# Attention scores from block 3 on as two 128-row products a head, with the key transposes moved to the first head's score bank

## Chip, core and metric

The program runs on one core of one Trainium2 chip. The metric is device time in microseconds (us), from three runs of the kernel before and one profiled execution of it. The inputs are fixed: 4 sequences of 768 tokens, 8 heads of 64 channels, two mixture layers behind the attention.

## What is computed

```python
scores = scale * np.matmul(q, k.transpose(0, 1, 3, 2))      # [4, 8, 768, 768], scale = 1/8
keep = is_sink | in_window                                  # first 4 keys, and the last 128 up to the query
scores = np.where(keep, scores, -1000000000.0)
a = np.exp(scores - np.max(scores, axis=-1, keepdims=True))
a = a / (np.sum(a, axis=-1, keepdims=True) + 1e-09)
x = np.matmul(a, v)                                         # heads side by side: [3072, 512]
...
h = np.maximum(x @ w_in, 0.0)                               # [3072, 2048]
x = h * h @ w_out                                           # [3072, 512]
...
out[mask] = gate_w[mask, None] * eom[mask, e, None] * (np.maximum(x[mask] @ w1[e], 0.0) @ w2[e])
```

The last line runs over 8 experts, each on the tokens whose largest gate logit is its own. The change touches the scores alone.

## The kernel before

**Stages.** The 3072 tokens are cut into 12 blocks of 256 (`t`), three to a sequence. While TensorE multiplies block t-1 by `w_in` (`l1`, L610) and `w_out` (`l2`, L635), sixteen pieces a block, the attention of block t runs in between (`attn_events`, L585). From about 730 us on the experts follow. Every product of the large matrices is made of three: each float32 operand is split into a high part and a rest, and high times high, high times rest and rest times high are added up in the accumulator.

**One attention step.** A block has 8 steps: four pairs of heads (`p`), two halves of 128 queries each (`n`). A step has four parts. `scores` (L446) multiplies the queries by 256 keys and 4 sink keys: 260 columns, or 128 in the first half of a sequence's first block. VectorE adds the mask and finds the maximum (L469), ScalarE exponentiates (L472) and scales (L484). `ptrans` (L492) transposes the probabilities on TensorE, ScalarE and VectorE split them (L512, L513), and GpSimd cuts them into the two key blocks (L517). `pv` (L523) multiplies them by the values. `prep_k` (L366) and `prep_q` (L395) bring the keys and queries of a pair into columns by transposes on TensorE, once for its two steps, and split them.

**The 64-row products.** A head has 64 channels, so a pair fills 128 rows, the first head on rows 0 to 63, the second on 64 to 127. From block 2 on (`T32`) a step's scores are three products for each head, in turns of first and second head, each over 64 rows:

```python
for m, (a_, b_) in enumerate(((0, 0), (0, 1), (1, 0)) if t >= T32 else ()):
    for e in range(2):
        r = slice(64 * e, 64 * e + 64)
        PE.matmul(ps[e][:, 0:W], lhsT=qt[r, a_, n, :], rhs=kt[r, b_, c0:c0 + W], start=(m == 0), stop=(m == 2))
```

**Accumulator banks.** `ps[0]` and `ps[1]` of a step lie in the banks `s0` and `s1`, one buffer each. The query transposes use `s0` too. The key transposes (`psk_`), the probabilities' (`pspt`), the sink sums' (`psst`, `fin_sink`, L557) and the gate's pieces (`psg`) share the one bank `T`. `pv` and the sink's correction (`add_sink`, L565) share the bank `O`.

**Order.** A sorted list of events sets where the attention's parts fall. A step's scores stand every fourth half-piece; `LEADS` (L36) says how far ahead of them the key and query transposes stand, and how far behind the probabilities' transposes and `pv`. `run_to` (L859) takes the due events once after each `l1` and once after each `l2`. A scheduler then sets the order on the other engines.

Of the kernel before, what the change touches and what calls it, by code (L numbers as in the profile page):

```python
# [8 lines left out]
F32 = mybir.dt.float32  # L9
F32R = mybir.dt.float32r  # L10
# [3 lines left out]
AF = mybir.ActivationFunctionType  # L14
ALU = mybir.AluOpType
# [31 lines left out]
def kern(ctx, tc, q, k, v, n_sink, window, w_in, w_out, w_gate, w_og, w1, w2, out):  # L47
    nc = tc.nc
    V, A, G, PE, SY = nc.vector, nc.scalar, nc.gpsimd, nc.tensor, nc.sync
# [16 lines left out]
    psS = ps1.enter_context(tc.tile_pool(name="psS", bufs=1, space=PSUM))  # L66
    psT = ps1.enter_context(tc.tile_pool(name="psT", bufs=1, space=PSUM))
# [7 lines left out]
    ident = const.tile([128, 128], F32, name="ident")  # L75
# [193 lines left out]
    att = attS.enter_context(tc.tile_pool(name="att", bufs=2, side="right"))  # L269
# [96 lines left out]
    def prep_k(t, p):  # L366
        o = 1 if t % 3 == 0 else 0
        x = nat.pop(("k", t, p))
        ps = psT.tile([128, 4, 128], F32, tag="T", name="psk_")
        if t == 0:  # L370
            fill(ps[:].rearrange("p n c -> p (n c)"), 1)
        for n in range(o, 3):
            PE.transpose(ps[:, n], x[:, n].rearrange("p h d -> p (h d)"), ident[:])
        kt = att.tile([128, 2, KS * 3], F32R, tag="kT", name="kT", bufs=2)
        kv = kt[:].rearrange("p a (n c) -> p a n c", c=KS)
        if t < T32:
            kf = kv[:, 0].bitcast(F32)
# [9 lines left out]
        A.activation(out=kv[:, 0, o:3, 0:128], in_=ps[:, o:3], func=AF.Copy)  # L387
        V.tensor_tensor(out=kv[:, 1, o:3, 0:128], in0=ps[:, o:3], in1=kv[:, 0, o:3, 0:128].bitcast(F32), op=ALU.subtract)
        if o:
            G.tensor_copy(out=sk[:, p], in_=kv[:, :, 1, 0:NS].bitcast(F32))  # L390
        for n in range(o, 2):
            G.tensor_copy(out=kv[:, :, n, 128:KS], in_=sk[:, p].bitcast(F32))
        kTt[t, p] = kt

    def prep_q(t, p):  # L395
        x = nat.pop(("q", t, p))
        if t < T32:
            ps = psO.tile([128, 4, 128], F32, tag="O", name="psq")
        else:
            ps = psS.tile([128, 260], F32, tag="s0", name="psq")[:, 0:256].rearrange("p (n c) -> p n c", n=2)  # L400
# [4 lines left out]
        o = att.tile([128, 2, 2, 128], F32R, tag="qT", name="qT", bufs=2)  # L405
        qTt[t, p] = o
        if t < T32:
            if p % 2:
                A.activation(out=o[:, 0].bitcast(F32), in_=ps[:, 0:2], func=AF.Copy)
            else:  # L410
                V.tensor_copy(out=o[:, 0].bitcast(F32), in_=ps[:, 0:2])
            Vt[t, p] = nat.pop(("v", t, p))
            more(t, p)
            return
        A.activation(out=o[:, 0], in_=ps[:, 0:2], func=AF.Copy)
        V.tensor_tensor(out=o[:, 1], in0=ps[:, 0:2], in1=o[:, 0].bitcast(F32), op=ALU.subtract)
# [29 lines left out]
    def scores(t, p, n):  # L446
        i = 2 * (t % 3) + n
        W = 128 if i == 0 else 260
        c0 = KS * n if i else KS
        mask = (M0, M1, M2)[min(i, 2)]  # L450
        qt = qTt[t, p]
        kt = kTt[t, p]
        if t == 0 and n % 2:
            ps = [psX.tile([128, 512], F32, tag=f"x{e}", name=f"psx{e}") for e in range(2)]
        else:
            ps = [psS.tile([128, 260], F32, tag=f"s{e}", name=f"pss{e}") for e in range(2)]
        if t == 0:
            fill(ps[0][:, 0:W], 2)
        for e in range(2 if t < T32 else 0):
            r = slice(64 * e, 64 * e + 64)  # L460
            PE.matmul(ps[e][:, 0:W], lhsT=qt[r, 0, n, :].bitcast(F32), rhs=kt[r, 0, c0:c0 + W].bitcast(F32), start=True, stop=True)
        for m, (a_, b_) in enumerate(((0, 0), (0, 1), (1, 0)) if t >= T32 else ()):
            for e in range(2):
                r = slice(64 * e, 64 * e + 64)
                PE.matmul(ps[e][:, 0:W], lhsT=qt[r, a_, n, :], rhs=kt[r, b_, c0:c0 + W], start=(m == 0), stop=(m == 2))  # L465
# [89 lines left out]
    skT = {}  # L555

    def fin_sink(t):  # L557
        ps = psT.tile([128, 4, 128], F32, tag="T", name="psst")
        for n in range(2):
            PE.transpose(ps[:, n], psk[n][:].rearrange("p h c -> p (h c)").bitcast(F32), ident[:])  # L560
        o = att.tile([128, 2, 128], F32R, tag="pskT", name="pskT", bufs=1)
        A.activation(out=o[:], in_=ps[:, 0:2], func=AF.Copy)
        skT[t] = o
# [21 lines left out]
    def attn_events(t):  # L585

        ev = []
        h0 = 32 * (t - 1) - 8
        a0, a1, a2, a3 = LEADS[min(t, 2)]
        for p in range(4):  # L590
            ev.append((h0 + 8 * p - a0, lambda p=p: prep_k(t, p)))
            ev.append((h0 + 8 * p - a1, lambda p=p: prep_q(t, p)))
        for n in range(8):
            ev.append((h0 + 4 * n, lambda n=n: scores(t, n // 2, n % 2)))
            ev.append((h0 + 4 * n + a2, lambda n=n: ptrans(t, n // 2, n % 2)))
            ev.append((h0 + 4 * n + a3, lambda n=n: pv(t, n // 2, n % 2)))
# [594 lines left out]
```

## Time and profile before

| | |
|---|---|
| median of 3 runs | 1150.73 us (1150.65 to 1150.94) |
| profiled execution, its own time | 1149.8 us |
| its span, first to last instruction | 1148.1 us |
| TensorE busy (matmuls) | 1120.3 us, 98% |
| VectorE, ScalarE, GpSimd busy | 727.9 us (63%), 637.6 us (56%), 417.0 us (36%) |
| granted TensorE clock, mean of the span | 0.995 |

PE stands for TensorE, PEld for its weight loads, DVE for VectorE, ACT for ScalarE, POOL for GpSimd. A matmul's busy time includes the way of its data through the array, so neighbouring matmuls overlap in the records: what one costs the next is read from start to start, not from its length. A share of the whole span mixes stages, so the stretch that the change touches has to be read for itself. L12 is line 12 of the kernel.

### The profile page before, as it was taken

To read this page: it belongs to the slowest core of one execution; us is meant where nothing else is said; L and a number is where in the kernel's file an instruction comes from. 1 tells how busy PE (TensorE), PEld (TensorE's weight loads), DVE (VectorE), ACT (ScalarE), POOL (GpSimd) and SP (SyncE) were. 2 spreads that over 40 slices of the span, in tenths; PEclk is the share of its full clock that TensorE was granted. 3 is DMA by queue.
4 is the path that set the end of the run, shared out by engine and by line. 5 is a ranking of instruction groups with operands and counts; after the bars stand their busy time and mean duration, and the time that the engine had idled before them with its cause. 6 is when DMAs were issued, how large, how long until landed. Compare 5 with 4: busy or idle time off the path is not lost. (4 is left out here: it accounts for less than half of the span.)

```text
span 1148.1 us, 23733 instructions
## 1 busy us (share of the span) xinstructions
PE 1120.3 (98%) x7002; PEld 941.3 (82%) x7002; DVE 727.9 (63%) x2027; ACT 637.6 (56%) x1749; POOL 417.0 (36%) x917
## 2 busy tenths in 40 slices
PE   7999999999999999999999999999999999999995
PEld 4556788888888888888888888997788888888884
DVE  4899877576766666676667676557412576764153
ACT  4898766777676767676767767454232232232200
POOL 3112563256564336565325655310211112221111
PEclk9999999999999999999999999999999999999998
DMA  6687111121211111211112110296411456653110
GB/s 154 179 234 211 39 24 46 39 54 34 54 29 50 38 45 38 56 28 44 36 38 56 38 31 1 28 253 162 129 39 47 155 185 218 220 206 134 48 45 24
DMA packets 139392, 100.08 MB, mean 87 GB/s; under 512 B 103908, under 2 KB 112228, under 8 KB 139239
## 3 DMA queue, kind: packets, MB, share of 16 engines
q1 hardware_dynamic: 131476, 82.28, 25.8%
q0 software_dynamic: 5472, 14.19, 3.7%
q10 hardware_dynamic: 2290, 1.84, 0.5%
q8 instruction: 64, 1.05, 0.4%
q14 instruction: 90, 0.73, 0.3%
HBM read 85.56 MB, written 13.76 MB: 87 GB/s over the span
## 5 line engine op out<-in xcount | busy, mean ns | idle before, releaser
L619 PE MATMUL psh<-xT,WI 128*128 128x256 f32 x2112 | 284.8, 285 | 0.0
L619 PEld LDWEIGHTS psh<-xT,WI 128*128 128x128 f32 x2112 | 270.6, 190 | 9.7 <-issue 0.4
L956 PE MATMUL psh<-WI,xt 128*128 (+1 forms) x672 | 162.1, 395 | 1.0 <-ACT xt L936 0.7
L629 DVE TENSOR_TENSOR r<-r 128x256 f32<-128x256 f32 x180 | 82.3, 458 | 116.8 <-ACT r L622 116.7
L644 PE MATMUL psx<-WOb,h 128*128 128x512 f32 x576 | 154.0, 404 | 0.8 <-ACT h L631 0.5
L956 PEld LDWEIGHTS psh<-WI,xt 128*128 128x128 f32 x672 | 123.8, 188 | 26.8 <-ACT xt L936 1.4
L644 PE MATMUL psx<-WOa,h 128*128 128x512 f32 x528 | 143.4, 406 | 0.0
L644 PEld LDWEIGHTS psx<-WOb,h 128*128 128x128 f32 x576 | 101.8, 188 | 19.9 <-ACT h L631 1.4
L472 ACT ACTIVATE P<-P,st 128x260 f32<-128x260 f32 (+1 forms) x192 | 93.8, 489 | 42.8 <-DVE st L469 42.7
L972 DVE TENSOR_TENSOR ht<-psht,ht 128x512 fp32r<-128x512 f32 x56 | 38.5, 689 | 120.7 <-ACT ht L936 120.3
L622 ACT ACTIVATE r<-psh 128x256 f32<-128x256 f32 x192 | 71.5, 372 | 66.1 <-PE psh L619 62.9
L644 PEld LDWEIGHTS psx<-WOa,h 128*128 128x128 f32 x528 | 92.7, 189 | 15.3
L517 POOL TENSOR_SCALAR_AFFINE_SELECT PT<-PT 128x256 fp32r<-128x256 f32 x224 | 98.4, 472 | 16.2 <-DVE PT L513 16.0
L994 POOL DMA_INDIRECT out_dram<-xg,pidx x28 | 28.7, 1024 | 198.8 <-ACT xg L993 158.0
L632 DVE TENSOR_TENSOR h<-r,h 128x256 fp32r<-128x256 f32 x184 | 83.8, 456 | 17.8 <-ACT h L631 12.0
L631 ACT ACTIVATE h<-r 128x256 fp32r<-128x256 f32 x184 | 76.1, 413 | 28.8 <-DVE r L629 24.4
L469 DVE CUSTOM_DVE_ANT_0 P<-pss,M 128x260 f32<-128x260 f32 (+1 forms) x184 | 72.7, 403 | 23.1 <-PE pss L465 11.3
L985 PE MATMUL psy<-WOb,ht 128*128 (+1 forms) x336 | 84.0, 398 | 0.0
L962 ACT ACTIVATE r<-psh 128x512 f32<-128x512 f32 x48 | 28.7, 598 | 98.6 <-PE psh L956 96.8
L985 PE MATMUL psy<-WOa,ht 128*128 (+1 forms) x336 | 82.2, 392 | 0.0
L484 ACT ACTIVATE P<-P,st 128x132 f32<-128x132 f32 (+2 forms) x168 | 62.2, 415 | 35.6 <-DVE st L475 35.4
L553 POOL TENSOR_TENSOR xr<-tB,tC 128x128 f32<-128x128 f32 x80 | 38.2, 478 | 103.1 <-DVE tB L552 98.3
(450 smaller groups left out, 1958.3 us busy)
## 6 DMA issues: line engine op xcount, KB each, us to landing
raw<-in_moe_w_dram SPq DMA_DIRECT2D x36, 1024.0 KB, 5.7
craw<-in_moe_w_out_dram SPq DMA_DIRECT2D x15, 512.0 KB, 4.0
craw<-in_moe_w_in_dram SPq DMA_DIRECT2D x14, 512.0 KB, 4.1
x2tab<-x2s SPq DMA_DIRECT2D x24, 256.5 KB, 3.1
kn<-in_k_dram SPq DMA_DIRECT2D x64, 96.0 KB, 2.2
vn<-in_v_dram SPq DMA_DIRECT2D x64, 96.0 KB, 2.2
qn<-in_q_dram SPq DMA_DIRECT2D x92, 64.0 KB, 2.1
kn<-in_k_dram SPq DMA_DIRECT2D x32, 64.0 KB, 2.0
```

The source lines that it names most:

```text
L469: V.tensor_tensor_reduce(out=P[:, e, 0:W], in0=ps[e][:, 0:W], in1=mask[:, 0:W], scale=-SCALE, scalar=3.0e38, op0=ALU.add, op1=ALU.min, acc ...
L472: A.activation(out=P[:, e, 0:W], in_=P[:, e, 0:W], func=AF.Exp, scale=-1.0, bias=st[:, e:e + 1], accum_out=st[:, 4 + e:5 + e])
L484: A.activation(out=P[:, e, 0:W], in_=P[:, e, 0:W], func=AF.Copy, scale=st[:, 6 + e:7 + e])
L517: G.affine_select(out=both[:, 1 - b, e], in_=bf[:, 0, e], pattern=[[0, 2], [1 - 2 * b, 128]], compare_op=ALU.is_gt if b else ALU.is_ge, fi ...
L619: PE.matmul(ps[:], lhsT=WI[:, j, a_, kk, :], rhs=x[:, b_, kk, :], start=(n == 0), stop=(n == 11))
L622: A.activation(out=hq[:], in_=ps[:], func=AF.Relu)
L629: E_.tensor_tensor(out=hq[:], in0=hq[:], in1=hq[:], op=ALU.mult)
L631: A.activation(out=o[:, 0], in_=hq[:], func=AF.Copy)
L632: V.tensor_tensor(out=o[:, 1], in0=hq[:], in1=o[:, 0].bitcast(F32), op=ALU.subtract)
L644: PE.matmul(acc[t][m][:], lhsT=o[:, a_, 128 * m:128 * m + 128], rhs=WO[j // 8][:, j % 8, b_, :], start=(j == 0 and n == 0), stop=(j == NF ...
L956: PE.matmul(ps[:], lhsT=o[:, a_, kk, :], rhs=wview(n, par + 2048 * b_ + 512 * kk, 512), start=(c == 0), stop=(c == 11))
L985: PE.matmul(yp[s][:], lhsT=o[:, a_, kk, :], rhs=wview(2 + n, par + 2048 * b_ + 512 * kk, 512), start=(n == 0 and kk == 0 and c == 0), stop ...
```

## The change

From block 3 on (`STK`) one tile `qst` holds a pair's queries in four pieces, and a head's scores are two products over all 128 rows. The first has the high query twice in its weights, on both halves of the rows, and on the other side the high key on the head's own half and the key's rest on the other: it gives high times high and high times rest. The second has the query's rest on the head's half and zeros on the other. ScalarE and VectorE write the pieces in two instructions of 64 rows where there was one of 128, VectorE's into the other half for the keys; GpSimd copies the high queries to the other half (two copies a pair), and writes the zeros once. `qst` is one buffer where the queries had two.

From block 3 on the key transposes use the bank `s0`, the sink sums' transposes the bank `s1`. The leads change: the key transposes stand one half-piece earlier, after `l2` and not after `l1`, and the probabilities' transposes of a step now stand ahead of the next step's scores.

```diff
-T32 = 2
-LEADS = ((5, 2, 4.5, 8.5), (5, 2, 4.5, 8), (5.5, 2.5, 4.5, 8))
+T32, STK = 2, 3
+HALF = (slice(0, 64), slice(64, 128))
+LEADS = ((5, 2, 4.5, 8.5), (5, 2, 4.5, 8), (5.5, 2.5, 4.5, 8), (6.5, 2.5, 3.95, 7.92))
...
     def prep_k(t, p):
-        ps = psT.tile([128, 4, 128], F32, tag="T", name="psk_")
+        if t < STK:
+            ps = psT.tile([128, 4, 128], F32, tag="T", name="psk_")
+        else:
+            ps = psS.tile([128, 512], F32, tag="s0", name="psk_")[:].rearrange("p (n c) -> p n c", n=4)
...
+            for e in range(2):
+                A.activation(out=kv[HALF[e], e, o:3, 0:128], in_=ps[HALF[e], o:3], func=AF.Copy)
+            for e in range(2):
+                V.tensor_tensor(out=kv[HALF[1 - e], e, o:3, 0:128], in0=ps[HALF[e], o:3], in1=kv[HALF[e], e, o:3, 0:128].bitcast(F32),
+                                op=ALU.subtract)
...
     def prep_q(t, p):
...
+            if "s" not in qbuf:
+                o = qbuf["s"] = att.tile([128, 2, 2, 2, 128], F32R, tag="qT", name="qst", bufs=1)
+                for e in range(2):
+                    r = HALF[1 - e]
+                    G.tensor_copy(out=o[r, 1, e].rearrange("p n (a c) -> p (n a) c", c=64),
+                                  in_=ident[r, None, 64 * e:64 * e + 64].broadcast_to([64, 4, 64]))
+            o = qbuf["s"]
+            qTt[t, p] = o
+            for e in range(2):
+                A.activation(out=o[HALF[e], 0, e], in_=ps[HALF[e], 0:2], func=AF.Copy)
+            for e in range(2):
+                V.tensor_tensor(out=o[HALF[e], 1, e], in0=ps[HALF[e], 0:2], in1=o[HALF[e], 0, e].bitcast(F32), op=ALU.subtract)
+            for e in range(2):
+                G.tensor_copy(out=o[HALF[1 - e], 0, e], in_=o[HALF[e], 0, e].bitcast(F32))
...
     def scores(t, p, n):
...
-        for m, (a_, b_) in enumerate(((0, 0), (0, 1), (1, 0)) if t >= T32 else ()):
+        for e in range(2 if t >= STK else 0):
+            for a_ in range(2):
+                PE.matmul(ps[e][:, 0:W], lhsT=qt[:, a_, e, n, :], rhs=kt[:, e, c0:c0 + W], start=(a_ == 0), stop=(a_ == 1))
+        for m, (a_, b_) in enumerate(((0, 0), (0, 1), (1, 0)) if T32 <= t < STK else ()):
...
     def fin_sink(t):
-        ps = psT.tile([128, 4, 128], F32, tag="T", name="psst")
+        if t < STK:
+            ps = psT.tile([128, 4, 128], F32, tag="T", name="psst")
+        else:
+            ps = psS.tile([128, 512], F32, tag="s1", name="psst")[:].rearrange("p (n c) -> p n c", n=4)
...
-        a0, a1, a2, a3 = LEADS[min(t, 2)]
+        a0, a1, a2, a3 = LEADS[min(t, 3)]
...
-            ev.append((h0 + 31, lambda: fin_sink(t)))
+            ev.append((h0 + (31 if t < STK else 31.91), lambda: fin_sink(t)))
```

What is left out of the diff keeps the queries of blocks 0 to 2 in the two halves of a tile that is named by stage.

The first place is TensorE around one step in block 7 that has key transposes behind it. `psh` is an `l1` piece, `psx0` and `psx1` an `l2` piece, `pso` is `pv`, `pspt` the probabilities' transposes, `pss0` and `pss1` the two heads' scores. Before (of the scores the first two rows; they stand there three times):

```order
L543 MATMUL pso_5073<-PT_4981,V_4753 128x256 x4
L465 MATMUL pss0_5086<-kT_4910,qT_4999 128x260
L465 MATMUL pss1_5087<-kT_4910,qT_4999 128x260
...
L501 MATMUL pspt_5108<-ident_102,P_4964 128x128 x2
L644 MATMUL psx0_4988<-WOa,h2_4940 128x512 x3
L644 MATMUL psx1_4989<-WOa,h2_4940 128x512 x3
L619 MATMUL psh_5124<-xT_1910,WI 128x256 x12
L373 MATMUL psk__5143<-ident_102,kn_4758 128x128 x3
```

Now:

```order
L578 MATMUL pso_5081<-PT_4966,V_4760 128x256 x4
L536 MATMUL pspt_5094<-ident_102,P_4979 128x128 x2
L496 MATMUL pss0_5104<-kT_4896,qst_2574 128x260 x2
L496 MATMUL pss1_5105<-kT_4896,qst_2574 128x260 x2
L682 MATMUL psx0_4993<-WOa,h2_4947 128x512 x3
L682 MATMUL psx1_4994<-WOa,h2_4947 128x512 x3
L378 MATMUL psk__5130<-ident_102,kn_4765 128x128 x3
L657 MATMUL psh_5141<-xT_1902,WI 128x256 x12
```

The scores are four products and not six, the probabilities' transposes stand ahead of them, and the key transposes one `l1` piece nearer to the scores whose bank they take.

The second place is VectorE in the same step. L469 (now L504) reads a head's scores, L513 (now L548) splits the probabilities, L388 (now L399) makes the rest of the keys. Before:

```order
L469 ISA P_5094,st_5095<-pss0_5086,M2_136 128x260
L469 ISA st_5095 128x1
L632 TENSOR_TENSOR h2_5070<-r_5067,h2_5070 128x256
L551 TENSOR_TENSOR tB_5078<-pso_5073,tB_5078 64x128
L552 TENSOR_TENSOR tB_5078<-pso_5073,tB_5078 64x128
L469 ISA P_5094,st_5095<-pss1_5087,M2_136 128x260
L469 ISA st_5095 128x1
L513 TENSOR_TENSOR PT_5111<-pspt_5108,PT_5111 128x2x128
...
L475 RECIPROCAL st_5095<-st_5095 128x2
L629 TENSOR_TENSOR r_5137<-r_5137 128x256
L388 TENSOR_TENSOR kT_5147<-psk__5143,kT_5147 128x3x128
```

Now:

```order
L504 ISA P_5110,st_5111<-pss0_5104,M2_136 128x260
L504 ISA st_5111 128x1
L670 TENSOR_TENSOR h2_5078<-r_5075,h2_5078 128x256
L586 TENSOR_TENSOR tB_5086<-pso_5081,tB_5086 64x128
L587 TENSOR_TENSOR tB_5086<-pso_5081,tB_5086 64x128
L548 TENSOR_TENSOR PT_5097<-pspt_5094,PT_5097 128x2x128
L504 ISA P_5110,st_5111<-pss1_5105,M2_136 128x260
L504 ISA st_5111 128x1
...
L510 RECIPROCAL st_5111<-st_5111 128x2
L399 TENSOR_TENSOR kT_5134<-psk__5130,kT_5134 64x3x128 x2
L667 TENSOR_TENSOR r_5154<-r_5154 128x256
```

The first head's read has kept its place; the split of the probabilities has moved ahead of the second head's, and the keys' rest is two instructions, ahead of the next `l1` piece's square (`r`).

The third place is GpSimd in the step before it, which has query transposes behind it. `PT` are the probabilities in key blocks, `psk1` the sink sums:

```order
L588 TENSOR_TENSOR xr_145<-tB_4955,tC_4956 128x128
L552 AFFINE_SELECT PT_4966<-PT_4966 128x256 x4
L448 CAST qst_2574<-qst_2574 64x256 x2
L522 CAST psk1_143<-P_4979 128x2x4
L523 CAST psk1_143<-P_4979 128x2x4
```

The two copies of the queries stand behind the four selects of the probabilities.

## Rows read from the trace of the kernel before

**Rows 1.** The page: span and busy time of the engines.

```profile
span 1148.1 us, 23733 instructions
...
PE 1120.3 (98%) x7002; PEld 941.3 (82%) x7002; DVE 727.9 (63%) x2027; ACT 637.6 (56%) x1749; POOL 417.0 (36%) x917
```

**Rows 2.** Busy us by stretch: length, PE, PEld, DVE, ACT, POOL (counts); clock, DMA share, GB/s.

```profile
176.00:720.00 544.00, 543.08 (x3940) 482.82 (x3939) 376.00 (x1311) 384.06 (x1177) 274.42 (x654) 1.00 0.16 40
488.00:495.59 7.59, 7.59 (x49) 6.45 (x49) 6.84 (x25) 5.59 (x19) 5.95 (x15) 1.00 0.17 38
```

**Rows 3.** TensorE's waits, 176 to 720 us: total us, times, longest us.

```profile
PE psc L754 <- DVE x2U L679: 0.4, 1, 0.4
PE psk__8745 L373 <- DVE PT L521: 0.2, 1, 0.2
```

**Rows 4.** Timeline of TensorE through one step: start us, us, what.

```profile
501.01 1.60 PE L619 MATMUL psh<-xT,WI 128*128 128x256 f32 x12
502.45 0.64 PE L543 MATMUL pso<-PT,V 128*128 128x256 f32 x4
503.02 0.63 PE L465 MATMUL pss<-kT,qT 64*128 64x260 f32 x6
503.58 0.44 PE L501 MATMUL pspt<-ident,P 128*128 128x128 f32 x2
503.77 1.64 PE L644 MATMUL psx<-WOa,h 128*128 128x512 f32 x6
505.25 0.38 PE L404 MATMUL psq<-ident,qn 128*128 128x128 f32 x2
505.39 1.67 PE L619 MATMUL psh<-xT,WI 128*128 128x256 f32 x12
506.90 0.27 PE L669 MATMUL psg<-ident,x2s 128*128 128x128 f32 x1
```

**Rows 5.** The same step in windows so short that single products stand apart.

```profile
502.81 0.28 PE L543 MATMUL pso<-PT,V 128*128 128x256 f32 x1
...
503.24 0.41 PE L465 MATMUL pss<-kT,qT 64*128 64x260 f32 x4
...
503.37 0.28 PE L465 MATMUL pss<-kT,qT 64*128 64x260 f32 x2
...
503.75 0.27 PE L501 MATMUL pspt<-ident,P 128*128 128x128 f32 x1
...
504.09 0.39 PE L644 MATMUL psx<-WOa,h 128*128 128x512 f32 x1
```

**Rows 6.** Timeline of TensorE through a step of 128 score columns.

```profile
540.74 0.64 PE L543 MATMUL pso<-PT,V 128*128 128x256 f32 x4
...
541.98 1.63 PE L644 MATMUL psx<-WOb,h 128*128 128x512 f32 x6
543.45 1.58 PE L619 MATMUL psh<-xT,WI 128*128 128x256 f32 x12
```

**Rows 7.** Groups by line on VectorE and GpSimd: xcount | busy us, mean ns.

```profile
L388 DVE TENSOR_TENSOR kT<-psk__8019,kT 128x384 fp32r<-128x384 f32 x1 | 0.6, 559 | 0.0
...
L416 DVE TENSOR_TENSOR qT<-psq,qT 128x256 fp32r<-128x256 f32 x30 | 12.1, 405 | 0.0
...
L422 POOL CAST V<-vn 128x192 fp32r<-128x192 f32 x44 | 18.6, 449 | 50.1 <-PE pso L543 50.1
```

**Rows 8.** Timeline of all engines behind one step's scores.

```profile
518.66 0.44 PE L501 MATMUL pspt<-ident,P 128*128 128x128 f32 x2
...
518.87 0.43 DVE L469 CUSTOM_DVE_ANT_0 P<-pss,M 128x260 f32<-128x260 f32 x1 [0.30 <-POOL V L422]
...
521.30 1.74 POOL L517 TENSOR_SCALAR_AFFINE_SELECT PT<-PT 128x256 fp32r<-128x256 f32 x4 [0.28 <-DVE PT L513]
```

**Rows 9.** Timeline at a block's end: the sink sums' transposes and their copy.

```profile
478.18 0.38 PE L560 MATMUL psst<-ident,psk 128*128 128x128 f32 x2
...
478.84 0.37 ACT L562 ACTIVATE pskT<-psst 128x256 fp32r<-128x256 f32 x1
```

More of the change, by code (lines that the diff above doesn't have):

```diff
@@ L333, in kern @@
     nat = {}
+    qbuf = {}
     qTt = {}
@@ L386, in prep_k @@
             return
-        A.activation(out=kv[:, 0, o:3, 0:128], in_=ps[:, o:3], func=AF.Copy)
-        V.tensor_tensor(out=kv[:, 1, o:3, 0:128], in0=ps[:, o:3], in1=kv[:, 0, o:3, 0:128].bitcast(F32), op=ALU.subtract)
+        if t < STK:
+            A.activation(out=kv[:, 0, o:3, 0:128], in_=ps[:, o:3], func=AF.Copy)
+            V.tensor_tensor(out=kv[:, 1, o:3, 0:128], in0=ps[:, o:3], in1=kv[:, 0, o:3, 0:128].bitcast(F32), op=ALU.subtract)
+        else:
[4 more added lines that the diff above has]
+                                op=ALU.subtract)
         if o:
@@ L399, in prep_q @@
         else:
[L400 removed]
+            ps = psS.tile([128, 512], F32, tag="s0", name="psq")[:, 0:256].rearrange("p (n c) -> p n c", n=2)
         if t == 0:
@@ L404, in prep_q @@
             PE.transpose(ps[:, n], x[:, n].rearrange("p h d -> p (h d)"), ident[:])
-        o = att.tile([128, 2, 2, 128], F32R, tag="qT", name="qT", bufs=2)
-        qTt[t, p] = o
+        if t < STK:
+            own = t // T32
+            if own not in qbuf:
+                qbuf[own] = att.tile([128, 2, 2, 2, 128], F32R if own else F32, tag="qT", name=f"qT{own}", bufs=1)
+            o = qbuf[own][:, p % 2]
+            qTt[t, p] = o
         if t < T32:
             if p % 2:
-                A.activation(out=o[:, 0].bitcast(F32), in_=ps[:, 0:2], func=AF.Copy)
+                A.activation(out=o[:, 0], in_=ps[:, 0:2], func=AF.Copy)
             else:
-                V.tensor_copy(out=o[:, 0].bitcast(F32), in_=ps[:, 0:2])
+                V.tensor_copy(out=o[:, 0], in_=ps[:, 0:2])
             Vt[t, p] = nat.pop(("v", t, p))
@@ L414, in prep_q @@
             return
-        A.activation(out=o[:, 0], in_=ps[:, 0:2], func=AF.Copy)
-        V.tensor_tensor(out=o[:, 1], in0=ps[:, 0:2], in1=o[:, 0].bitcast(F32), op=ALU.subtract)
+        if t < STK:
+            A.activation(out=o[:, 0], in_=ps[:, 0:2], func=AF.Copy)
+            V.tensor_tensor(out=o[:, 1], in0=ps[:, 0:2], in1=o[:, 0].bitcast(F32), op=ALU.subtract)
+        else:
+            if "s" not in qbuf:
[5 more added lines that the diff above has]
+            o = qbuf["s"]
+            qTt[t, p] = o
+            for e in range(2):
[4 more added lines that the diff above has]
+                G.tensor_copy(out=o[HALF[1 - e], 0, e], in_=o[HALF[e], 0, e].bitcast(F32))
         n0 = 1 if t % 3 == 0 else 0
@@ L455, in scores @@
         else:
-            ps = [psS.tile([128, 260], F32, tag=f"s{e}", name=f"pss{e}") for e in range(2)]
+            ps = [psS.tile([128, 512], F32, tag=f"s{e}", name=f"pss{e}") for e in range(2)]
         if t == 0:
@@ L460, in scores @@
             r = slice(64 * e, 64 * e + 64)
-            PE.matmul(ps[e][:, 0:W], lhsT=qt[r, 0, n, :].bitcast(F32), rhs=kt[r, 0, c0:c0 + W].bitcast(F32), start=True, stop=True)
-        for m, (a_, b_) in enumerate(((0, 0), (0, 1), (1, 0)) if t >= T32 else ()):
+            PE.matmul(ps[e][:, 0:W], lhsT=qt[r, 0, n, :], rhs=kt[r, 0, c0:c0 + W].bitcast(F32), start=True, stop=True)
+        for e in range(2 if t >= STK else 0):
+            for a_ in range(2):
+                PE.matmul(ps[e][:, 0:W], lhsT=qt[:, a_, e, n, :], rhs=kt[:, e, c0:c0 + W], start=(a_ == 0), stop=(a_ == 1))
+        for m, (a_, b_) in enumerate(((0, 0), (0, 1), (1, 0)) if T32 <= t < STK else ()):
             for e in range(2):
@@ L557, in fin_sink @@
     def fin_sink(t):
-        ps = psT.tile([128, 4, 128], F32, tag="T", name="psst")
+        if t < STK:
+            ps = psT.tile([128, 4, 128], F32, tag="T", name="psst")
+        else:
+            ps = psS.tile([128, 512], F32, tag="s1", name="psst")[:].rearrange("p (n c) -> p n c", n=4)
         for n in range(2):
```

## The prediction

> **What bounds the kernel now.** I read the page first, then the busy time of the stretch that the change touches, then what TensorE waits for there, then the timeline of single steps. TensorE is busy for 98% of the span [rows 1], but that mixes stages. From 176 to 720 us, blocks 3 to 11, it is busy for 543.08 of 544.00 us at the full granted clock, while VectorE has 376, ScalarE 384 and GpSimd 274 us of work [rows 2]. Its waits there come to about 1 us: 0.4 us for the gate, and three of 0.2 us of key transposes for VectorE, which has to empty the bank `T` first (one of the three is shown) [rows 3]. So the time of this stretch is the sum of what TensorE's products cost from start to start. What makes that sum smaller by 1 us makes the kernel faster by 1 us, as long as the other engines keep up; what lengthens their work costs nothing until one comes late.
>
> **What one step costs now.** Behind the `l1` piece come `pv`, the scores, the probabilities' transposes and the `l2` piece [rows 4]. `pv` starts at 502.45 us, the scores at 503.02, the transposes at 503.58, `l2` at 503.77 and what follows it at 505.25: 2.80 us from `pv` to the end of `l2`. In shorter windows [rows 5] the reader sees that the six score products start as three pairs, at 503.02, 503.24 and 503.37, two heads at once. A pair therefore costs about 0.12 us once it runs, but three places cost more than that. The last product of `pv` starts at 502.81 and the first pair 0.21 us later, though a 256-column product costs 1.44 / 12 = 0.120 us in the `l1` piece of 501.01 [rows 4]. The second pair starts 0.22 us after the first. The last pair starts at 503.37 and the transposes 0.21 us later. And the first transpose costs 0.17 us (503.58 to 503.75). I read the excess of 0.09, 0.10 and 0.09 us as the price of going from 128-row products to 64-row ones, of the second set of weights there, and of going back.
>
> **What it costs then.** Nothing of 64 rows is left from block 3 on. By row: `pv`, four products of 0.120, is 0.48 us. Two transposes cost 0.105 us each: from the query transposes at 505.25 to the end of the next `l1` piece at 506.90 are 1.65 us, less 1.44 [rows 4]. A score product of 260 columns and 128 rows has no row. Its nearest is the 256-column product, so 0.122 us and 0.49 for four. `l2` without a disturbance in front is 6 times 0.232 (504.09 to 505.25 are five products [rows 4, 5]), 1.39 us. Together 0.48 + 0.21 + 0.49 + 1.39 = 2.57 against 2.80: 0.23 us a step. Counted from the four excesses (0.09 + 0.10 + 0.09 + 0.06) less the longer scores (0.49 - 3 x 0.12 = 0.13) it is 0.21. I take 0.22.
>
> **The sum.** Nine blocks of 8 steps are 72. In 60 the scores have 260 columns: 60 x 0.22 = **13.2 us**. In the 12 of blocks 3, 6 and 9 with n = 0 they have 128. There `pv` to the end of `l2` is 2.71 us (540.74 to 543.45 [rows 6]). Four 128-column products cost between 0.105 each (the transposes, also 128 columns) and 0.122, so the step then takes 2.50 to 2.57 us and saves 0.14 to 0.21. I take 0.20, since the transposes have the same column count: 12 x 0.20 = **2.4 us**. The three waits for the bank `T` go, as the keys no longer use it: **0.6 us** [rows 3]. The key transposes are as many as before, and stand between the same two kinds of product in the other order: nothing. Gain 16.2 us.
>
> **What is added, and what hides it.** VectorE does the keys' rest twice on 64 rows and the queries' too. L388 takes 0.56 us, L416 0.41 [rows 7], and if half the rows don't make them shorter, 36 pairs add 36 x 0.97 = 35 us to 376 in 529: 78% busy. ScalarE does as much more. GpSimd copies 64 x 256 values twice a pair. By L422 (0.45 us for 192 columns [rows 7]) I estimate 0.5 us each, 36 us on 274. TensorE's own work hides these, 7 us of it between one step and the next; without that cover they would cost all of the 35 us.
>
> The bank `s0` now passes through four hands in a pair: scores, key transposes, scores, query transposes. The key transposes come 0.49 + 1.39 = 1.88 us after the scores' start. Before, VectorE began to read the scores 0.21 us after the probabilities' transposes, that is 0.77 after the scores' start, and took 0.51 [rows 4, 8]. The first head's two products now come first, so its read should end about 1.2 us after the start: 0.7 us to spare. The queries' copies stand behind the four selects on GpSimd, which end 4.38 us after the probabilities' transposes (521.30 + 1.74 - 518.66 [rows 8]). The next scores start some 7.4 + 0.2 us after those transposes (a step of 7.59 [rows 2] less 0.22), so two copies have 3.2 us.
>
> Thin places are at a block's end. The sink sums' copy on ScalarE ends 1.03 us after the transposes' start (478.18 to 479.21 [rows 9]). These now sit in `s1`, and the second head's scores want it 0.21 + 0.48 + 0.21 + 0.24 = 1.14 us after that start: 0.1 us to spare. The first sink correction now stands behind two 0.56 us instructions and a square on VectorE, and `pv` waits for its bank. Only blocks 4, 5, 7, 8, 10 and 11 have these two waits: nothing at best, at worst about 1.1 us a block (two more of L388), 6.6 in all. I take 0.2 a block, **1.2 us**, near the lower end, because both come out with something to spare.
>
> Net 16.2 - 1.2 = **15.0 us**. The profiled execution took 1149.8 us itself, 1.7 more than its span, and would take 1134.8. The median of the runs lies 0.9 above it: 1150.7 - 15.0 = **1135.7 us**.
>
> **Rivals.**
>
> *The other engines come late at the block changes.* In the step from 488.00 to 495.59 VectorE is busy for 6.84 of 7.59 us [rows 2]. With 0.41 more in a step 0.22 shorter it has 7.25 of 7.37. If 0.7 us of this reaches TensorE in each of nine blocks, 6 us are lost: about 1142. For it: the margin is 0.1 us. Against it: TensorE waits for nothing there now, and the split of a block lies a piece ahead of its use.
>
> *The bank s0 is handed over late (slower).* If VectorE's read of the first head ends more than 0.7 us later than I have it, TensorE waits in each of 72 steps. From 0.7 + 15.0 / 72 = 0.9 us late there is no gain left; at 1 us late it is 1150.7 + 72 x 0.3 - 15.0 = 1157. For it: one buffer, and a queue in which the read stands behind a square that waits for ScalarE. Against it: the order on VectorE keeps that read where it was, and the query transposes had the same hand-over in 36 steps without one wait [rows 3].
>
> *Two rows at once were the better use (slower).* If the excess at the pairs' edges belongs to something else and stays, the change sets four products for three pairs: 0.13 us more in 72 steps, 9.4 less 0.6, so 1159.5. For it: each pair does run in 0.12 us [rows 5]. Against it: all three excesses stand exactly at the 64-row products, and the same transposes behind an `l2` piece have none [rows 4]. The Trainium skill, TensorEngine Tiling (Array Packing), Theoretical Speedup, speaks for this rival: a contraction of 64 or less gains up to twice from being packed into separate tiles, which is what the change gives up. By that rule alone the 1159.5 would hold.
>
> **How the numbers follow.** 0.2% of this kernel (2.3 us) is about what a measurement can tell from no change. My forecast, 1133 to 1138, has 78%. Its lower end is 0.23 and 0.21 us a step without a new wait (13.8 + 2.5 + 0.6 = 16.9), its upper end the thin places at half their worst. The first rival, 1138 to 1145, has 14%, s0 4%, the packed rows 3%, and 1% is that waits use up the gain just so. The range of 1133 to 1142 leaves out the upper part of the first rival, the slower cases and a little below. Faster: 0.92; the same: 0.02; slower: 0.06.
>
> **What would show it.** Right: `pv` to the end of `l2` at 2.57 us in the timeline, the score products single and 0.12 us apart, no 0.2 us at their edges, and TensorE still without waits outside the blocks' ends. The first rival shows as waits of TensorE for the accumulator of the scores or of `pv`, the second as waits of the key transposes for L504, the third as gaps that stay at the score products. I am wrong if a 128-row score product costs 0.15 us or more, or if TensorE's waits from block 3 on exceed 6 us.

## The result, and the profile after

The changed kernel takes 1158.68 us (median of 6 runs, 1157.95 to 1161.9), the one before 1151.13 (6 runs). The ratio is 1.0066, 95% interval 1.0056 to 1.0077: 0.7% slower, where 1135.7 us was forecast. The profiled execution took 1157.95 us, its span is 1156.2 for 1148.1, so 8.1 us have to be found.

The same stretch as in [rows 2], in the busy times by stretch of the changed kernel (length, PE, PEld, DVE, ACT, POOL, clock, DMA share, GB/s):

```profile
176.00:720.00 544.00, 529.32 (x3774) 482.38 (x3773) 427.28 (x1378) 417.23 (x1241) 296.02 (x720) 1.00 0.16 40
```

TensorE, busy for 543.08 us of it before, now has 15 us without work. The other engines have more: VectorE 51 us, ScalarE 33, GpSimd 22. The waits of TensorE that answer to [rows 3], same columns, from the list for 170 to 730 us:

```profile
PE psk__3402 L378 <- DVE st L504: 1.6, 1, 1.6
PE psk__3190 L378 <- DVE st L504: 1.6, 1, 1.6
...
PE psst L598 <- DVE pf L733: 1.1, 1, 1.1
PE psk__5627 L378 <- DVE st L504: 1.0, 1, 1.0
PE psk__8515 L378 <- DVE st L504: 0.8, 1, 0.8
```

Six waits of 1.6 us and seven smaller ones, 13.2 us in all, are of one kind: key transposes that want `s0` and wait for VectorE's read of the scores in it (L504, L469 before). All of them lie in or next to blocks 3, 6 and 9.

The step itself became what was priced. TensorE's timeline of the changed kernel through a step with 260 columns:

```profile
513.50 0.65 PE L578 MATMUL pso<-PT,V 128*128 128x256 f32 x4
513.98 0.38 PE L536 MATMUL pspt<-ident,P 128*128 128x128 f32 x2
514.12 0.72 PE L496 MATMUL pss<-kT,qst 128*128 128x260 f32 x4
514.68 1.54 PE L682 MATMUL psx<-WOa,h 128*128 128x512 f32 x6
516.05 0.49 PE L378 MATMUL psk__8018<-ident,kn 128*128 128x128 f32 x3
```

From `pv` to the end of `l2` it is 2.55 us (513.50 to 516.05), 2.80 before [rows 4], 2.57 forecast; over the 54 steps with 260 columns whose four parts stand side by side in the trace the median is 2.56, before 2.79. In shorter windows the second, third and fourth score product start at 514.32, 514.44 and 514.56, and `l2` 0.12 us after the last; the 0.2 us edges of [rows 5] are gone. The 0.20 us behind the first product (514.12) are no edge: its start is recorded only 0.03 us after that of the transpose before it (514.09), and the two together cost 0.23.

Where the 8.1 us arise, by the same marks in both traces: 1.1 ahead of block 3's first scores (176.47, now 177.57); 2.5 from there to the last scores (715.93, now 719.51), instead of a gain of 15; and about 5 at the start of the experts. Elsewhere the two differ by less than 0.4.

**One late hand-over**, in block 3, in the changed kernel's timeline of all engines (a bracket gives the idle time before, and what ended it):

```profile
207.02 0.60 PE L536 MATMUL pspt<-ident,P 128*128 128x128 f32 x4
...
207.38 0.64 PE L496 MATMUL pss<-kT,qst 128*128 128x128 f32 x4
...
207.70 1.17 POOL L719 TENSOR_TENSOR x2U<-x2U,x2T 128x512 bf16<-128x512 f32 x1 [4.04 <-issue]
...
207.85 1.61 PE L682 MATMUL psx<-WOa,h 128*128 128x512 f32 x6
207.88 1.28 DVE L667 TENSOR_TENSOR r<-r 128x256 f32<-128x256 f32 x1 [0.97 <-ACT r L660]
...
209.07 0.27 DVE L586 TENSOR_TENSOR tB<-pso,tB 64x128 f32<-64x128 f32 x1
209.19 0.42 ACT L669 ACTIVATE h<-r 128x256 fp32r<-128x256 f32 x1 [0.50 <-DVE r L667]
209.36 0.29 DVE L587 TENSOR_TENSOR tB<-pso,tB 64x128 f32<-64x128 f32 x1
209.51 0.58 ACT L555 ACTIVATE PT<-pspt 128x512 fp32r<-128x512 f32 x1
209.69 0.43 DVE L670 TENSOR_TENSOR h<-r,h 128x256 fp32r<-128x256 f32 x1
...
210.15 0.69 DVE L556 TENSOR_TENSOR PT<-pspt,PT 128x512 fp32r<-128x512 f32 x1
210.75 0.28 DVE L504 CUSTOM_DVE_ANT_0 P<-pss,M 128x128 f32<-128x128 f32 x1
...
211.10 0.44 PE L378 MATMUL psk__3190<-ident,kn 128*128 128x128 f32 x2 [1.63 <-DVE st L504]
```

The scores start at 207.38, and about 2 us later `l2` is through and the key transposes could start. The read stands at 210.75, behind five other instructions of VectorE. The last of these, L556, splits four transposes at once, 512 columns: in the blocks that begin a sequence the probabilities of every second step come in two key blocks for each head, and behind such a step stands one with 128 score columns. Over the trace, the first head's read ends 1.06 us (median) after the scores' start where they have 260 columns, and 3.34 us after it in the twelve steps with 128.

The split is not all of it. The first of the five, the square L667, takes 1.28 us here and 0.43 in the median: it starts 0.18 us behind GpSimd's L719, a piece of the gate, and ends after it (last section). ScalarE's L669 waits 0.50 us for it, and L555, L556 and the read follow on that. All six waits of 1.6 us stand behind such a square, of 1.28 or 1.29 us; in their steps the read ends 3.65 us after the scores' start. The first steps of blocks 4, 7 and 10 have 260 columns, the same split in front and a square of 0.42 us: there the read ends 3.05 us after it, and the wait is 0.43. From these rows I estimate that 0.5 to 0.6 us of each wait of 1.6 us is the longer square; no run shows these steps without it.

**The start of the experts.** SyncE's and TensorE's timelines before:

```profile
807.92 5.80 SPq L923 DMA_DIRECT2D pidx<-perm  x6
```

```profile
811.13 2.88 PE L985 MATMUL psy<-WOb,ht 128*128 128x512 f32 x12
814.38 0.66 PE L942 MATMUL psxt<-ident,xg 128*128 128x128 f32 x4 [0.37 <-DMA xg<-x2tab,pidx]
...
821.58 0.60 PE L942 MATMUL psxt<-ident,xg 128*128 128x128 f32 x4
```

And after:

```profile
811.04 7.36 SPq L961 DMA_DIRECT2D pidx<-perm  x6
```

```profile
814.39 2.88 PE L1023 MATMUL psy<-WOb,ht 128*128 128x512 f32 x12
820.05 1.12 PE L980 MATMUL psxt<-ident,xg 128*128 128x128 f32 x4 [2.78 <-DMA xg<-x2tab,pidx]
...
829.77 0.60 PE L980 MATMUL psxt<-ident,xg 128*128 128x128 f32 x4
```

The products `psy` are 3.3 us behind the kernel before, the expert's first transposes 5.7, the next ones 8.2. First the indices (`pidx`) come late: the gather on GpSimd that waits for them starts 5.64 us after their issue, 2.86 before. Then TensorE is at its lower level. The changed kernel's busy times by stretch, columns as above:

```profile
819.90:826.80 6.90, 6.06 (x16) 4.56 (x17) 4.12 (x3) 0.60 (x1) 0.98 (x2) 0.51 0.65 222
```

The granted clock is 0.51 (the level of 1.2 GHz) for 6.9 us behind that wait. Just behind the issue of `pidx` lies the one packet of an instruction queue in the changed kernel's DMA view of 811 to 817 us; 3.2% of 16 engines over 6 us are 3.07 us for this one packet of 16 KB:

```profile
q8 instruction: 1, 0.02, 3.2%
```

### The profile page after: what moved, and what is told of

It reads as the page before. It is cut to its first block, busy times and chain, and to the rows that moved or that the text cites. A ratio compares the mean times of both kernels' runs of the same rounds, so it can differ in the third digit from the quotient of the medians.

```text
span 1156.2 us, 23964 instructions
## 1 busy us (share of the span) xinstructions
PE 1112.5 (96%) x6858; PEld 945.9 (82%) x6858; DVE 783.0 (68%) x2099; ACT 673.7 (58%) x1821; POOL 438.5 (38%) x991
## 5 line engine op out<-in xcount | busy, mean ns | idle before, releaser
L657 PE MATMUL psh<-xT,WI 128*128 128x256 f32 x2112 | 288.5, 285 | 0.0
L682 PE MATMUL psx<-WOb,h 128*128 128x512 f32 x576 | 150.2, 397 | 0.8 <-ACT h L669 0.4
L682 PE MATMUL psx<-WOa,h 128*128 128x512 f32 x528 | 140.2, 401 | 0.0
L667 DVE TENSOR_TENSOR r<-r 128x256 f32<-128x256 f32 x180 | 96.7, 538 | 44.6 <-ACT r L660 42.9
L669 ACT ACTIVATE h<-r 128x256 fp32r<-128x256 f32 x184 | 75.7, 412 | 49.6 <-DVE r L667 46.6
L552 POOL TENSOR_SCALAR_AFFINE_SELECT PT<-PT 128x256 fp32r<-128x256 f32 x224 | 92.3, 447 | 3.8 <-DVE PT L548 3.7
L504 DVE CUSTOM_DVE_ANT_0 P<-pss,M 128x260 f32<-128x260 f32 (+1 forms) x184 | 71.7, 398 | 12.0 <-PE pss L500 3.4
L1023 PEld LDWEIGHTS psy<-WOa,ht 128*128 128x128 f32 x336 | 62.6, 188 | 12.9
```

Of the source, the lines that this page charges most:

```text
L504: V.tensor_tensor_reduce(out=P[:, e, 0:W], in0=ps[e][:, 0:W], in1=mask[:, 0:W], scale=-SCALE, scalar=3.0e38, op0=ALU.add, op1=ALU.min, acc ...
L552: G.affine_select(out=both[:, 1 - b, e], in_=bf[:, 0, e], pattern=[[0, 2], [1 - 2 * b, 128]], compare_op=ALU.is_gt if b else ALU.is_ge, fi ...
L657: PE.matmul(ps[:], lhsT=WI[:, j, a_, kk, :], rhs=x[:, b_, kk, :], start=(n == 0), stop=(n == 11))
L667: E_.tensor_tensor(out=hq[:], in0=hq[:], in1=hq[:], op=ALU.mult)
L669: A.activation(out=o[:, 0], in_=hq[:], func=AF.Copy)
L682: PE.matmul(acc[t][m][:], lhsT=o[:, a_, 128 * m:128 * m + 128], rhs=WO[j // 8][:, j % 8, b_, :], start=(j == 0 and n == 0), stop=(j == NF ...
```

## The experiments

All were run beside the kernel before, whose median was 1151.1 to 1151.5 us. I cite block lengths (from a block's first scores to the next one's) by the two kinds of blocks; they come from each kernel's trace.

| kernel | blocks 3, 6, 9 | 4, 5, 7, 8, 10 | last scores at | median us | ratio, 95% interval |
|---|---|---|---|---|---|
| before | 60.8 | 60.8 | 715.9 | 1151.13 | |
| changed | 64.0 | 59.6 | 719.5 | 1158.68 | 1.0066 [1.0056, 1.0077] |
| e1 stacked products alone | 60.0 | 63.9 | 732.2 | 1168.46 | 1.0146 [1.0112, 1.0179] |
| e2 moves alone | 66.0 | 65.3 | 757.1 | 1192.59 | 1.0353 [1.0321, 1.0384] |
| e3 keys later | 62.0 | 60.7 | 719.8 | 1158.92 | 1.0066 [1.0040, 1.0092] |
| e4 old step order | 62.0 | 61.9 | 730.6 | 1165.01 | 1.0100 [1.0067, 1.0133] |
| e5 mixed order | 60.2 | 59.6 | 708.1 | 1143.35 | 0.9934 [0.9917, 0.9951] |
| e6 halves alone | 61.1 | 62.0 | 724.7 | 1159.45 | 1.0075 [1.0058, 1.0091] |
| e7 small fills | 64.0 | 59.6 | 719.9 | 1154.08 | 1.0027 [1.0016, 1.0039] |
| e8 mixed order, small fills | 60.2 | 59.6 | 708.7 | 1144.23 | 0.9945 [0.9928, 0.9961] |
| e9 new order, keys in T | 63.4 | 61.2 | 728.5 | 1162.86 | 1.0102 [1.0086, 1.0118] |
| e10 mixed order, later sink | 61.1 | 59.6 | 708.7 | 1143.26 | 0.9929 [0.9918, 0.9941] |
| e11 mixed the other way | 63.9 | 63.4 | 743.7 | 1179.40 | 1.0234 [1.0216, 1.0251] |

**e1, the stacked products alone.**

```diff
-LEADS = (..., (6.5, 2.5, 3.95, 7.92))
+LEADS = (..., (5.5, 2.5, 4.5, 8))
...
-        if t < STK:
-            ps = psT.tile([128, 4, 128], F32, tag="T", name="psk_")
-        else:
-            ps = psS.tile([128, 512], F32, tag="s0", name="psk_")[:].rearrange("p (n c) -> p n c", n=4)
+        ps = psT.tile([128, 4, 128], F32, tag="T", name="psk_")
...
-            ev.append((h0 + (31 if t < STK else 31.91), lambda: fin_sink(t)))
+            ev.append((h0 + 31, lambda: fin_sink(t)))
```

(`psst` goes back to `T` in the same way.)

> The changed kernel with its stacked products and its new query buffers, but with everything that it moved put back: key and sink transposes in bank T, at their old places, probabilities' transposes behind the scores. Theory A (the moves cause the waits): TensorE's waits from block 3 to the last scores fall from about 17.7 us to under 4, and the stretch from the first scores of block 3 to the last scores of block 11 is 12 to 15 us shorter than in the kernel before. Time 1136 to 1139 us if the start of the experts goes as before, 1141 to 1144 if the 5 us lost there stay. Rival B (the added copies and halved operations on ScalarE, VectorE and GpSimd make the engines late in any order): at least 10 us of waits stay, time 1147 us or more. Rival C (the loss lies outside the stretch, at the start of the experts): the stretch is no better than in the changed kernel, time 1151 to 1158.

1168.46 us: theory A, which I held, falls, and what B gave (10 us of waits at least, 1147 us or more) came. Blocks 3, 6 and 9 are 0.8 us shorter than before, as if nothing waited; the others are 3.1 longer. The waits are in another bank. From e1's timeline in block 4:

```profile
268.04 1.17 POOL L713 TENSOR_TENSOR x2U<-x2U,x2T 128x512 bf16<-128x512 f32 x1 [1.27 <-ACT x2T L712]
268.21 1.29 DVE L661 TENSOR_TENSOR r<-r 128x256 f32<-128x256 f32 x1 [0.64 <-ACT r L654]
...
268.54 0.38 PE L533 MATMUL pspt<-ident,P 128*128 128x128 f32 x2
...
270.15 1.60 PE L651 MATMUL psh<-xT,WI 128*128 128x256 f32 x12
...
271.27 0.36 ACT L544 ACTIVATE PT<-pspt 128x256 fp32r<-128x256 f32 x1
...
272.09 0.42 DVE L545 TENSOR_TENSOR PT<-pspt,PT 128x256 fp32r<-128x256 f32 x1
...
272.57 0.55 PE L375 MATMUL psk__4160<-ident,kn 128*128 128x128 f32 x3 [0.82 <-DVE PT L545]
```

The probabilities' transposes enter `T` at 268.54, VectorE has emptied it only at 272.51, and the key transposes wanted it when `l1` ended at 271.75. In the kernel before the median from those transposes to the end of their split is 2.52 us where the probabilities come packed, here 3.44. The long square is in this step too (L661 here, L713 on GpSimd): all eleven waits of the key transposes in e1, of 0.8 to 0.9 us, stand behind one of 1.28 or 1.29 us. So the new order of the step is no ornament: it hides the added work of VectorE and ScalarE where the probabilities come packed.

**e2, the moves alone**: the kernel before with the new leads, `s0` for the keys, `s1` for the sink sums, and its 64-row products.

```diff
-LEADS = ((5, 2, 4.5, 8.5), (5, 2, 4.5, 8), (5.5, 2.5, 4.5, 8))
+LEADS = ((5, 2, 4.5, 8.5), (5, 2, 4.5, 8), (5.5, 2.5, 4.5, 8), (6.5, 2.5, 3.95, 7.92))
```

> The kernel before, its 64-row triple products kept, with only the moves made: key transposes in s0, sink transposes in s1, the four new leads, the sink's later place. Theory A: the waits of the key transposes for VectorE's read of s0 appear here too in blocks 3, 6 and 9, without any of the added copies; 10 to 18 us of waits, time 1160 to 1168 us. Rival B (the added work is the cause): no wait over 0.5 us on the key transposes, time 1149 to 1153. Rival C: the moves cost nothing in the stretch, 1149 to 1153, unless the start of the experts is hit, then 1156.

1192.59 us, far over what A gave. The waits for `s0` are there without one added copy, but in all blocks, and the query transposes have them too (e2's list of waits):

```profile
PE psq L408 <- DVE st L473: 11.0, 33, 0.4
PE psk__6279 L377 <- DVE st L473: 1.2, 1, 1.2
```

The first head's read ends 2.8 us (median) after the scores' start. VectorE has it behind the split of the probabilities here, in packed steps too; from e2's timeline of VectorE, behind scores that start at 281.91:

```profile
284.04 0.42 DVE L517 TENSOR_TENSOR PT<-pspt,PT 128x256 fp32r<-128x256 f32 x1
284.38 0.42 DVE L473 CUSTOM_DVE_ANT_0 P<-pss,M 128x260 f32<-128x260 f32 x1
```

With 64-row products in turns the first head is done only with the fifth of six products; that this is why the read comes later on VectorE was not tried. The moves need the stacked products as much as those need the moves.

**e3, the keys a step later**: `LEADS[3] = (5.5, 2.5, 3.95, 7.92)`.

> The changed kernel with one of its numbers back: the key transposes a whole step later (lead 5.5 for 6.5), still in s0; the probabilities' transposes stay ahead of the scores. Theory A: the hand-over of s0 behind l2 is still there, now behind another step, so the waits of 1.6 us in blocks 3, 6 and 9 shift to the next step or shrink to 0.5 to 1.6 us: time 1147 to 1158 us. Rival B: nothing changes, 1157 to 1160. Rival C: nothing changes in the stretch.

1158.92 us. The key transposes' waits shrink to six of 0.2 us, and the scores now wait for the keys' rest (e3's list of waits):

```profile
PE pss L496 <- DVE kT L399: 9.6, 23, 0.9
```

Blocks 3, 6 and 9 gain 2.0 us each, the others lose 1.1. The sum only looks like no change, and lies 0.9 us above what A gave. The loss at the start of the experts is in it as in the changed kernel (a wait of 3.26 us there).

**e4, the old order within the step**: `LEADS[3] = (6.5, 2.5, 4.5, 8)`, the keys still in `s0`.

> The changed kernel with the probabilities' transposes and the query transposes back at their old places in the step (third and fourth leads 4.5 and 8); keys stay in s0 and one step early. Theory A, if the order of probabilities and scores on VectorE is what makes the read of s0 late: the six waits of 1.6 us on the key transposes fall under 0.5 each, waits of the stretch 3 to 7 us, time 1139 to 1148. Theory A, if the bank alone does it: they stay, time 1155 to 1160. Rival B: 1155 or more. Rival C: stretch as in the changed kernel.

Neither figure of A: the key transposes' waits are gone from the list, as its first half says, yet it takes 1165.01 us, as B gave (1155 or more). Both kinds of blocks take 62 us in the mean; the largest waits are of the gate's transposes for `T` (5.9 us in 12, as in e1) and of the scores for the sink sums' copy (3.4 us in 5). The order decides who is late: the scores' read if the probabilities' transposes stand ahead of the scores, the probabilities' split if they stand behind.

**e5, each order where it fits.**

```diff
-        if t < STK:
+        if t < STK or t % 3 == 0:
             ps = psT.tile([128, 4, 128], F32, tag="T", name="psk_")
...
-        a0, a1, a2, a3 = LEADS[min(t, 3)]
+        a0, a1, a2, a3 = LEADS[min(t, 3)] if t % 3 else LEADS[min(t, 2)]
```

> The changed kernel, but blocks 3, 6 and 9 (whose probabilities come unpacked) keep the old order and the old bank for their keys; blocks 4, 5, 7, 8, 10 and 11 have the new one. By the runs before, blocks 3, 6, 9 took 63.4 to 64.4 us each in the changed kernel and 60.0 with the stacked products alone, the other six 59.6 in the changed kernel and 63.9 with the stacked products alone (60.8 in the kernel before). Theory D (each order suits one kind of block, and the losses don't move elsewhere): blocks 3 to 11 together 10 us shorter than in the changed kernel, last scores at 709 to 711 us; time 1144 to 1148 us, or 1140 to 1143 if the 5 us lost at the start of the experts don't come. Rival E (the work added to VectorE and ScalarE costs about 10 us somewhere in any order): no better than 1153.

1143.35 us, 0.66% faster than the kernel before and 1.3% than the changed one. Theory D held: last scores at 708.1, a little under its range, and the loss at the experts did not come, for which D gave 1140 to 1143, 0.35 us less. TensorE's two longest groups of waits from 177 to 716 us in e5:

```profile
PE psg L707 <- DVE PT L556: 1.1, 3, 0.4
PE psv L470 <- DVE pf L733: 1.0, 3, 0.3
```

**e6, the halved operations alone**, in the kernel before:

```diff
-        A.activation(out=kv[:, 0, o:3, 0:128], in_=ps[:, o:3], func=AF.Copy)
+        for r in (slice(0, 64), slice(64, 128)) if t >= 3 else (slice(0, 128),):
+            A.activation(out=kv[r, 0, o:3, 0:128], in_=ps[r, o:3], func=AF.Copy)
```

and so for the keys' rest and for both operations of the queries.

> The kernel before with its 64-row products, order and banks, where from block 3 on the keys' and queries' copies on ScalarE and rests on VectorE are each made in two halves of 64 rows. Nothing else of the change. Theory D (it is this added work of VectorE and ScalarE that makes the old order fail in blocks 4, 5, 7, 8, 10, 11, not the stacked products): key transposes wait for bank T as they do with the stacked products alone, six blocks of 61.5 to 64 us for 60.8, 1155 to 1170 us. Rival F (TensorE's shorter step alone makes the others late): no new waits, 1150 to 1153 us.

1159.45 us, within D's range: work of VectorE and ScalarE that I had called hidden costs 8.3 us in the old order, 1.2 in each of the blocks where the probabilities are packed. But it does not show as D said. The key transposes wait for `T` for 0.6 us, as in the kernel before; other waits in the list add 2.8 us (the sink sums' transposes 1.4, the probabilities' 0.8, the gate 0.6), and the rest are starts that slip by too little for it.

**e7, the code fetch moved.**

```diff
-    fill(psT.tile([128, 512], F32, tag="T", name="psi")[:], 12)
+    psi = psT.tile([128, 512], F32, tag="T", name="psi")
+    fill(psi[:, 0:128], 48)
```

> The changed kernel, with the 12 idle products of 512 columns at its start written as 48 of 128: the same columns into a bank that nobody reads, 36 products more, in front of a stretch in which TensorE is idle for 2.2 us. It moves each later fetch of TensorE's code to an earlier place of the program. If the 16 KB packet of the fetch at 811.7 us makes the read of the experts' indices late (theory G), the wait of 2.8 us at the start of the experts falls under 1.2, the granted clock stays at 1.00 there, and the time falls by 4 to 5 us: 1153 to 1155. If the fetch is not the cause (rival H), the wait stays and the time is 1157 to 1160.

1154.08 us, by theory G. The attention is the same to 0.4 us; the fetch that was at 811.7 us is at 804.2, which e7's DMA view of 803.8 to 808 us shows,

```profile
q8 instruction: 1, 0.02, 2.1%
```

and e7's timeline of TensorE reads as that of the kernel before:

```profile
814.70 2.88 PE L1024 MATMUL psy<-WOb,ht 128*128 128x512 f32 x12
818.61 0.66 PE L981 MATMUL psxt<-ident,xg 128*128 128x128 f32 x4 [1.02 <-DMA xg<-x2tab,pidx]
...
825.82 0.60 PE L981 MATMUL psxt<-ident,xg 128*128 128x128 f32 x4
```

So 4.6 us of the 7.6 that the changed kernel loses by the medians are lost at the start of the experts, not in the attention, and come back when the code is fetched elsewhere. That the packet itself holds up the read of the indices is the likely link, told by the times alone: in eleven of the thirteen traces the gather starts 2.86 to 2.88 us after the issue of the indices, and in the other two, the changed kernel and e3, 5.64 and 5.70 us after it. Only in these two does such a packet start within 0.7 us behind that issue (0.69 and 0.45 us). In e5 one lies 2.1 us behind it (802.3 and 800.17) and costs nothing.

**e8, e5 and e7 together.**

> Both together: old order in blocks 3, 6 and 9, and 48 small idle products at the start. Theories D and G: 1140 to 1144 us, 10 to 15 us below the changed kernel and 7 to 11 below the one before. D without G: as the mixed order alone. E: no better than 1149.

1144.23 us, as e5: D without G, for there was nothing left to win.

**e9, the new order with the keys in `T`.** `prep_k` as in e1, the leads as in the changed kernel.

> The changed kernel with its new order, but the key transposes in bank T again instead of s0. Theory I (in blocks 3, 6 and 9 the order is at fault: the four unpacked transposes and their 512-wide rest stand ahead of the scores' read on VectorE, so any bank comes late): those blocks stay at 62 us or more, now waiting for the rest of the probabilities; the other six 59.5 to 60.5; 1152 to 1160 us. Rival J (the bank s0 alone is at fault): blocks 3, 6, 9 fall to 60 to 60.5 us, the other six unchanged: 1142 to 1149 us, and s0 was never needed.

Theory I, in the blocks that it was about: 63.4 us. The same step as in the fence of the hand-over waits for L553 (L556 there), which stands just ahead of the scores' read (e9's list of waits for 177 to 241 us):

```profile
PE psk__3402 L375 <- DVE PT L553: 1.4, 1, 1.4
PE psk__3190 L375 <- DVE PT L553: 1.4, 1, 1.4
```

The other blocks came out at 61.2, over the 59.5 to 60.5 expected: there `s0` is worth 1.6 us a block, and the time of 1162.86 lies above the range.

**e10, the sink transposes of block 2 later**: `31 if t < T32 else 31.91` in e5.

> The kernel with the mixed order, and the sink transposes of block 2 a piece later, as those of block 4 on already are. TensorE waits 1.17 us for the bank before them, at 174 us. If the bank is free by then: 1.0 to 1.5 us below the mixed order alone, 1141.5 to 1142.5 us; if the wait only moves to the first correction that needs those sums: no change, 1143 to 1144.

1143.26 us: no change. The wait at 174 us is gone, and block 3 is 2.0 us longer: just behind its first scores the probabilities' transposes now wait 1.1 us for the copy of the sink sums.

**e11, the mixture the wrong way round**: both conditions of e5 turned over.

> The mixed order the wrong way round: new order and bank s0 in blocks 3, 6 and 9, old order and bank T in the other six. If block lengths simply add (3 of about 64 us and 6 of about 63.9 for 60.8, theory D): last scores at 742 to 746 us, 1174 to 1180 us. If the losses depend on what the neighbouring block does rather than on the kind of block: under 1168.

1179.40 us, last scores at 743.7: both within theory D, so the lengths of the two kinds of blocks do add.

## Why the prediction was wrong

**What a step costs** was right: 2.55 us for 2.57, with the scores of the two heads apart and no edges. The third rival is out: with the second set of weights and the two changes of row count, six 64-row products were not the better use here. The Trainium skill, TensorEngine Tiling (Array Packing), Theoretical Speedup, gives up to twice for packing a contraction of 64 rows or less; the trace agrees for the pairs themselves, two products in 0.12 us [rows 5], and not for the step as a whole.

**The step that failed is "What is added, and what hides it", at the bank `s0`.** "its read should end about 1.2 us after the start: 0.7 us to spare" holds for most steps of 260 columns (median 1.06). I took it from one such step [rows 8] and spread it over all. In the steps of 128 columns the read was late in the kernel before too, 2.51 us (median) behind the scores' start; nobody waited for it then. Its timeline of VectorE, behind the narrow step of [rows 6], whose scores start at 541.31:

```profile
542.48 0.43 DVE L632 TENSOR_TENSOR h<-r,h 128x256 fp32r<-128x256 f32 x1 [0.70 <-ACT h L631]
542.83 0.28 DVE L551 TENSOR_TENSOR tB<-pso,tB 64x128 f32<-64x128 f32 x1
543.13 0.29 DVE L552 TENSOR_TENSOR tB<-pso,tB 64x128 f32<-64x128 f32 x1
543.46 0.29 DVE L469 CUSTOM_DVE_ANT_0 P<-pss,M 128x128 f32<-128x128 f32 x1
```

That read, 2.44 us behind the scores' start, put against the 1.88 us after which the key transposes come, would have shown a wait of about 0.6 us. (The 0.51 us that the prediction gives to a read of 260 columns is 0.43 in [rows 8]; nothing hangs on it.) The second rival named the right mechanism and had 4%; its price was for 72 steps, while in truth six steps in three blocks lose 1.6 us each, and that its 1157 lies near the measured time is luck, as 4.6 us of that are lost elsewhere. Its "against it" (the order on VectorE keeps that read where it was) was true of the steps that I had looked at, and false in blocks 3, 6 and 9, where the split of 512 columns now stands ahead: with the old order these waits go (e4), and with the new order and another bank they stay (e9). The prediction also took VectorE's instructions at the lengths they had; in the six steps the square in front of the read takes 0.85 us more than its median.

**"TensorE's own work hides these"** was wrong as a statement on all orders: the halves alone cost 8.3 us (e6). The sizes were right: halves are no shorter (0.56 us for the keys, 0.42 for the queries), ScalarE got 33 us for the 35 forecast. VectorE got 51 for 35, since a line that the change does not touch became slower (last section).

**The thin places at the block ends** were put at 1.2 us; the sink sums do not appear among the changed kernel's waits from block 3 on. The first rival (engines late at block changes) is not what happened to it, though e5, without the hand-over, comes out near that rival's 1142.

**The sum**: if the 16.2 us of gain are taken as forecast, 18.7 were lost in the stretch, which became 2.5 longer. 13.8 of them are listed waits, more than the 6 that I had set as the mark of being wrong; about 5 are starts that slip too little for the list, and stay without a cause of their own. The experts' start had no term at all. Without these key transposes' waits, in e5, the stretch gains 9.1 of the 15.0 us (539.4 to 530.3 us from block 3's first scores to the last). The 1.1 us ahead of block 3 are TensorE's wait of 1.11 us before block 2's sink transposes (175.41): the `l2` piece before it starts at 172.67 us, and at 172.78 in the kernel before, so a fall of the clock at 137 us, in the changed kernel's profile alone of the two, has no part in them. Why VectorE is late there stays open; e10 moves the wait without a gain.

## What to carry to other kernels

Check the hand-over of a bank at every kind of step in the stretch, not at one typical step: the margin is from the taker's start to the last reader's end, and the reader's place in its engine's queue, and the length of what stands in front of it, differ where the data has another shape or another stage runs beside it. When an edit has two parts that each lose alone (e1, e2), look for the kind of block in which the pair still loses, and give that kind its own order. And when code is removed, compare also the stages behind it: a few microseconds there may come from where the program's fetches now fall.

## What the hardware did that I had not expected

The square of the `l1` pieces on VectorE (L667, L629 before) is the same work in both kernels. Its summary by line for 176 to 720 us, after and before (count, then duration in ns as least/median/greatest):

```profile
L667 DVE TENSOR_TENSOR r<-r x143: 398/427/1287, 177.8 to 719.5; 128x256 f32<-128x256 f32 x143
```

```profile
L629 DVE TENSOR_TENSOR r<-r x143: 397/426/877, 176.5 to 716.0; 128x256 f32<-128x256 f32 x143
```

The median has not moved; the mean went from 464 to 563 ns, 14 us in the stretch. 30 of the 143 take over 0.6 us, 11 before. In the fence of the hand-over one of them starts at 207.88, while GpSimd's L719 runs from 207.70 to 208.87, and ends at 209.16, 0.29 us after it, having taken 1.28 us. In the kernel before the square of that step started 0.86 us behind the same GpSimd instruction (206.82 and 205.96) and took 0.58 us; the change brought the two together. 17 of the 30 start while L719 runs, and each of them ends 0.28 us after it, whether it took 0.68 or 1.29 us. By the Trainium skill, SBUF — State Buffer, "SBUF: two separate sides", VectorE and GpSimd share a pair of ports that the one that comes first keeps for its whole instruction, also where a VectorE operation with two SBUF inputs meets a GpSimd operation that reads SBUF. These rows agree. No run took GpSimd's work away.

TensorE's granted clock fell to 0.51 behind its wait of 2.78 us at the experts' start, and is 1.00 over the stretch with the six waits of 1.6 us.
